# Last two output scatters issued without a wait between them, and the weight-conversion units of the second layer put into other steps of a block

## The chip, the core and the metric

The kernel runs on one core of one Trainium2 chip, as one launch. The metric is the device time of that launch in microseconds (us). Five engines work side by side, each through its own instructions in order: TensorE (PE, matmuls, with PEld for its weight loads), VectorE (DVE), ScalarE (ACT), GpSimd (POOL) and SyncE (SP). The letter q behind an engine's name means its sequencer: waits, branches and the issue of DMAs.

## The reference

Attention with two sparse masks, then a routed layer (each token goes to one of 8 experts), then a dense layer, in float32:

```
attn = softmax(where(mask, q k^T / 8, -1e9)) v           # 4 x 8 heads, 576 positions, 64 wide
x    = attn, heads side by side                          # 2304 tokens x 512
e    = argmax(x w_gate + bias[modality]);  x[e] = gate * relu(x[e] w1[e]) w2[e]
h    = x w_in                                            # 512 -> 2048
out  = where(h > 0, h, exp(min(h, 0)) - 1) w_out         # 2048 -> 512
```

The change touches only the last line, called the second layer here.

## The kernel before

**Stages.** The attention comes first (to about 100 us), then the routed layer (to about 396 us), then the second layer (to about 804 us). All matmul operands are split into a high and a low part, so one product is three matmuls: high by high, low by high, high by low. The splitting costs an ACT copy (the high part) and a DVE subtraction (the low part) for each operand tile.

**The second layer.** The tokens lie in five groups: groups 0 to 3 of 512 tokens and group 4 of 256. The 2048 hidden columns are worked in 16 chunks of 128. Ten blocks follow each other, named p = 0 to 9 here: p 0 to 4 take the groups in the order 0, 1, 4, 2, 3 with chunks 0 to 7, and p 5 to 9 take them in the order 3, 2, 1, 0, 4 with chunks 8 to 15. So each block has eight steps, c = 0 to 7, one chunk each; j counts the steps of all blocks.

A step does in program order, for each engine:
- `up`: twelve matmuls into a PSUM tile h_ps (L736 to L738), three ACT functions of it (t, e, r: L745 to L747), two DVE operations (L748, L749), the ACT copy gh (L750) and the DVE subtraction gl (L751), which are the operands of `down`;
- where they fall due: the split of a weight chunk (ACT wh L460, DVE wl L461) and of the next block's tokens (`prep`: ACT xh L449, DVE xl L450, in even steps);
- possibly one conversion unit (below);
- `down` of the step two before: twelve matmuls (six for group 4) that add into the output tiles o_ps (L772 to L774).

In the step that ends a block's `down`, the o_ps tiles are copied out of PSUM: by ACT (L781) and DVE (L783) in turn for p 0 to 4, and stored to a scratch array part_dram by a POOL DMA. Since `down` runs two steps late, the copies of block p are emitted at the end of step c = 1 of block p + 1, and the first `down` matmul of block p + 1, one step later, needs the PSUM bank that ACT's first copy frees. For p 5 to 9 DVE adds the scratch part to o_ps (L787), and a POOL indirect DMA scatters the 128 rows into the output (L788). There are 18 such scatters; each is made to wait until the one before it has landed, as all write the same array.

**Conversion units.** The weights w_in and w_out come as 64-bit numbers and are made 32-bit floats by 32 pieces of work in a software pipeline. A call of `conv.unit()` with number n stores piece n - 3 (SP DMA, L151), finishes piece n - 2 (DVE L144, L146), takes the bits of piece n - 1 apart (ACT cv_r L133, cv_a L134; DVE cv_t L136, L137) and loads piece n (SP, L119 or L122). The stages run on the same tiles, so within a unit ACT's cv_a waits for DVE's L146. Two pieces make one weight chunk. 23 units run during the routed layer, the others in the second layer, for p 0, 1, 3 and 4 (p 2 is the narrow group 4). Chunks 8 to 15 are read back by SP from step c = 3 of p = 4 on (L539), five steps ahead of their use.

**Order.** It is written out by hand: instructions stand on each engine in the order in which the code emits them, and a pool of buffers adds the waits. A wait holds everything behind it on its engine.

Of the kernel before, what the change touches and what calls it, by code (L numbers as in the profile page):

```python
# [36 lines left out]

def moe_attention_kernel(tc, q, k, v, mod, mbias, wg, w1, w2, w_in, w_out, out):
    nc = tc.nc
    with ExitStack() as ctx, tc.manual_schedule():  # L40
        const = ctx.enter_context(tc.tile_pool(name="const", bufs=1))
        dram = ctx.enter_context(tc.tile_pool(name="dram", bufs=1, space=DRAM))
        psum = ctx.enter_context(tc.tile_pool(name="psum", bufs=1, space=PSUM))
        x_dram = dram.tile([T, DM], F32, name="x_dram")
        conv = Conv(tc, dram, w_in, w_out)
        ident = const.tile([128, 128], F32, name="ident")

        def bank(tag, name, *shape):

            t = psum.tile([128, 512], F32, tag=tag, bufs={"S": 2, "T": 2, "P": 4}[tag], name=name)  # L50
            if not shape:
                return t
            n = 1
            for d in shape[1:]:
                n *= d
            t = t[0:shape[0], 0:n]
            if len(shape) == 3:
                t = t.rearrange("p (a b) -> p a b", a=shape[1])
            return t

        router = Router(tc, const, bank)
        part_dram = dram.tile([NT, 128, DM], F32, name="part_dram")
        ffn(tc, ctx, x_dram, part_dram, ident, router, conv, bank, w1, w2, out,
            lambda bg: attention(tc, bg, q, k, v, mod, mbias, wg, x_dram, ident, router, bank))


class Background:
# [29 lines left out]
class Conv:  # L97
# [51 lines left out]
    def store(self, n):  # L149
        f, part = divmod(n, 2)  # L150
        self.tc.nc.sync.dma_start(self.w[f, :, part * 512:(part + 1) * 512], self.done.pop(n))  # L151
# [245 lines left out]
def ffn(tc, ctx, x_dram, part_dram, ident, router, conv, bank, w1, w2, out, run_attention):  # L397
    nc = tc.nc
# [5 lines left out]
    idx, gate, idxd = router.idx, router.gates, router.idxd  # L404
# [114 lines left out]
    order = [0, 1, 4, 2, 3, 3, 2, 1, 0, 4]  # L519
# [27 lines left out]
    def fetch_to(g):  # L547
        while loaded[0] <= g:
            s, f = divmod(loaded[0], NCH)
            if s < NS:  # L550
                if s == len(jobs):
                    new_job(s)
                raws[loaded[0]] = fetch(jobs[s], f)
            else:
                fetch2(loaded[0] - NG)
            loaded[0] += 1

    def split_to(g):
        while splits[0] <= g:
            if splits[0] < NG:  # L560
                split_w(splits[0] % NW, raws.pop(splits[0]))
            else:
                split2(splits[0] - NG)
            splits[0] += 1
# [8 lines left out]
    def prep(p, kks=range(4)):  # L573
        s = order[p]
        for kk in kks:
            split_x(y_sb[0][:, kk, s * 512:s * 512 + widths[s]], yT[sets[p]][kk])
# [152 lines left out]
    def up(j):  # L729
        p, c = seq[j]  # L730
        i, n = where[j], widths[order[p]]
        ps = bank("ST"[j % 2], "h2_ps")[:, 0:n]
        for kk in range(4):
            a, b = (w[i][:, kk * 128:(kk + 1) * 128] for w in (WH, WL))
            yh, yl = (y[:, 0:n] for y in yT[sets[p]][kk])
            nc.tensor.matmul(ps, lhsT=a, rhs=yh, start=kk == 0, stop=False)  # L736
            nc.tensor.matmul(ps, lhsT=a, rhs=yl, start=False, stop=False)  # L737
            nc.tensor.matmul(ps, lhsT=b, rhs=yh, start=False, stop=kk == 3)  # L738

        t = e_p.tile([128, 512], F32, tag="t", name="t")[:, 0:n]  # L740
        e = e_p.tile([128, 512], F32, tag="e", bufs=1, name="e")[:, 0:n]
        r = e_p.tile([128, 512], F32, tag="r", name="r")[:, 0:n]
        gh = h_p.tile([128, 512], F32R, tag="hh", name="gh")
        gl = h_p.tile([128, 512], F32R, tag="hl", name="gl")
        nc.scalar.activation(t, ps, AF.Tanh, scale=0.5)  # L745
        nc.scalar.activation(e, ps, AF.Exp)  # L746
        nc.scalar.activation(r, ps, AF.Relu)  # L747
        nc.vector.scalar_tensor_tensor(t, e, 1.0, t, ALU.add, ALU.mult)  # L748
        nc.vector.scalar_tensor_tensor(r, t, 0.0, r, ALU.min, ALU.add)  # L749
        nc.scalar.copy(gh[:, 0:n], r)  # L750
        nc.vector.tensor_tensor(gl[:, 0:n], r, gh[:, 0:n].bitcast(F32), ALU.subtract)  # L751
        hid[j] = (gh, gl)

    parts = {}

    def load_part(p, m):

        parts[m] = xg_p.tile([128, DM], F32, tag="xg", name="part")
        nc.sync.dma_start(parts[m], part_dram[4 * order[p] + m])

    def down(j):
        p, c = seq[j]
        i, s = where[j], order[p]
        gh, gl = hid.pop(j)
        nt = widths[s] // 128
        first, last = j % HC == 0, j % HC == HC - 1
        if first:
            acc[p] = [bank("P", f"o_ps{m}") for m in range(nt)]
        for m in range(nt):
            a, b = (g[:, m * 128:(m + 1) * 128] for g in (gh, gl))  # L770
            ps = acc[p][m]
            nc.tensor.matmul(ps, lhsT=a, rhs=WH[i][:, 512:1024], start=first, stop=False)  # L772
            nc.tensor.matmul(ps, lhsT=a, rhs=WL[i][:, 512:1024], start=False, stop=False)  # L773
            nc.tensor.matmul(ps, lhsT=b, rhs=WH[i][:, 512:1024], start=False, stop=last)  # L774
            if not last:
                continue
            col = 4 * s + m
            if p < 5:
                o = xg_p.tile([128, DM], F32, tag="xg", name="o")
                if m % 2:  # L780
                    nc.scalar.copy(o, ps)  # L781
                else:
                    nc.vector.tensor_copy(o, ps)  # L783
                nc.gpsimd.dma_start(part_dram[col], o)
            else:
                o = parts.pop(m)
                nc.vector.tensor_tensor(o, ps, o, ALU.add)  # L787
                nc.gpsimd.indirect_dma_start(out, bass.IndirectOffsetOnAxis(idxd[:, col:col + 1], 0), o, None)  # L788

    fetch_to(NG + LAG - 1 + AHEAD)  # L790
    for j in range(NX + LAG):
        if j < NX:
            up(j)
            split_to(NG + j + SPLIT + 1)
            fetch_to(NG + j + AHEAD + 1)
            p, c = seq[j][0], j % HC
            if p + 1 < len(order) and sets[p + 1] != sets[p] and c % 2 == 0:
                prep(p + 1, [c // 2])
            if p < 5 and order[p] != 4 and c % 2 == 1:
                conv.unit()  # L800
            if p >= 5 and c >= 4 and c - 4 < widths[order[p]] // 128:
                load_part(p, c - 4)
        if j >= LAG:
            down(j - LAG)


def attention(tc, bg, q, k, v, mod, mbias, wg, x_dram, ident, router, bank):
# [333 lines left out]
```

## Time and profile before

| | us |
|---|---|
| median of 3 runs | 812.84 (810.42 to 813.59) |
| the profiled execution, device time | 815.83 |
| its span, first to last instruction | 814.1 |
| PE busy in the span | 775.6 (95%) |
| DVE busy | 517.0 (64%) |
| ACT busy | 397.0 (49%) |
| POOL busy | 105.3 (13%) |
| mean granted TensorE clock | 0.976 of full |

The device time is 1.73 us longer than the span. A matmul row of the timeline shows its start and its modelled length; since matmuls are pipelined, the distance from one start to the next tells more than the length. In a bracket behind a row stands how long the engine was idle before it and what ended that idle time.

### The profile page before, as it was taken

The numbers are of one execution on the slowest core, as the hardware profiler recorded it, in microseconds if no ns is written. First come the engines' busy times: TensorE is split into PE (matmuls) and PEld (weight loads), VectorE is DVE, ScalarE is ACT, GpSimd is POOL, SyncE is SP. The second block draws the span as 40 slices with busy tenths as digits, with TensorE's granted clock in tenths as the row PEclk, the third lists the DMA queues.
The fourth block names the chain that finished last, engine by engine and source line by source line (L and its number), as shares of the span: only waits on it lengthen the run. The fifth ranks groups of instructions, "written<-read, shape, count | busy, mean of one in ns | idle before, by whom it ended". The sixth has DMA issues, their size and how long they took to land.

```text
span 814.1 us, 12741 instructions
## 1 busy us (share of the span) xinstructions
PE 775.6 (95%) x4513; PEld 645.1 (79%) x4513; DVE 517.0 (64%) x1394; ACT 397.0 (49%) x759; POOL 105.3 (13%) x131
## 2 busy tenths in 40 slices
PE   7999989998999999999699899999999999999994
PEld 6899877776888888888587688788887888888884
DVE  3789878696867676765677656664467454545452
ACT  4667646422445453453466555554466444444341
POOL 4533342022002020000000101001001010101011
PEclk9999969999999999999899999999999999999998
DMA  9487692345556664555432222111133020211111
GB/s 171 116 184 179 148 239 66 107 139 153 201 188 200 203 221 157 183 181 164 148 103 79 95 74 91 39 45 75 37 103 130 1 93 11 66 39 47 57 39 64
DMA packets 100302, 94.37 MB, mean 116 GB/s; under 512 B 45433, under 2 KB 78731, under 8 KB 100235
## 3 DMA queue, kind: packets, MB, share of 16 engines
q1 hardware_dynamic: 95056, 78.79, 33.5%
q0 software_dynamic: 4480, 14.68, 5.2%
q8 instruction: 37, 0.61, 0.3%
q14 instruction: 30, 0.25, 0.1%
q10 hardware_dynamic: 699, 0.04, 0.1%
HBM read 70.95 MB, written 22.54 MB: 115 GB/s over the span
## 4 chain that ended last, share of the span: by engine, by line
PE 43%; DVE 4%; ACT 3%; issue 1%; DMA 0%; POOLq 0%; DVEq 0%; ACTq 0%
PE o_ps L772 7%; PE o_ps L774 7%; PE o_ps L773 7%; PE h_ps L736 7%; PE h_ps L737 7%; PE h_ps L738 7%; DVE r L749 1%; DVE t L748 1%; ACT gh L750 1%; DVE wl L461 1%; ACT t L745 1%; ACT e L746 1%; DVE cv_r L146 1%; ACT wh L460 0%; DVE cv_r L144 0%
## 5 line engine op out<-in xcount | busy, mean ns | idle before, releaser
L736 PE MATMUL h_ps<-xh,wh 128*128 128x512 f32 (+1 forms) x320 | 119.5, 373 | 6.8 <-DVEq L697 6.8
L748 DVE SCALAR_TENSOR_TENSOR t<-e,t 128x512 f32<-128x512 f32 (+1 forms) x80 | 51.1, 639 | 117.7 <-ACT e L746 117.7
L737 PE MATMUL h_ps<-xl,wh 128*128 128x512 f32 (+1 forms) x320 | 119.3, 373 | 0.3 <-DVE xl L450 0.3
L738 PE MATMUL h_ps<-xh,wl 128*128 128x512 f32 (+1 forms) x320 | 119.1, 372 | 0.0
L772 PE MATMUL o_ps<-wh,gh 128*128 128x512 f32 x288 | 113.9, 396 | 4.2 <-ACT o L781 4.2
L773 PE MATMUL o_ps<-wl,gh 128*128 128x512 f32 x288 | 113.4, 394 | 0.0
L774 PE MATMUL o_ps<-wh,gl 128*128 128x512 f32 x288 | 113.3, 394 | 0.0
L745 ACT ACTIVATE t<-h_ps 128x512 f32<-128x512 f32 (+1 forms) x80 | 44.3, 554 | 107.0 <-PE h_ps L738 107.0
L750 ACT CAST gh<-r 128x512 fp32r<-128x512 f32 (+1 forms) x80 | 46.2, 577 | 80.6 <-DVE r L749 80.6
L751 DVE TENSOR_TENSOR gl<-r,gh 128x512 fp32r<-128x512 f32 (+1 forms) x80 | 51.1, 639 | 51.5 <-ACT gh L750 51.5
L461 DVE TENSOR_TENSOR wl<-wraw,wh 128x1024 fp32r<-128x1024 f32 x56 | 68.6, 1225 | 13.7 <-ACT wh L460 12.4
L736 PEld LDWEIGHTS h_ps<-xh,wh 128*128 128x128 f32 x320 | 60.6, 189 | 19.3 <-issue 7.2
L737 PEld LDWEIGHTS h_ps<-xl,wh 128*128 128x128 f32 x320 | 60.7, 190 | 12.5 <-DVE xl L450 0.6
L738 PEld LDWEIGHTS h_ps<-xh,wl 128*128 128x128 f32 x320 | 60.5, 189 | 11.0
L772 PEld LDWEIGHTS o_ps<-wh,gh 128*128 128x128 f32 x288 | 54.5, 189 | 16.9 <-ACT o L781 5.1
L495 PE MATMUL y_ps<-hh,wh 128*128 128x512 f32 x160 | 64.3, 402 | 0.0
L476 PE MATMUL h_ps<-xh,wh 128*128 128x512 f32 x160 | 64.2, 401 | 0.0
L774 PEld LDWEIGHTS o_ps<-wh,gl 128*128 128x128 f32 x288 | 54.4, 189 | 12.3
L478 PE MATMUL h_ps<-xh,wl 128*128 128x512 f32 x160 | 63.6, 398 | 0.0
L773 PEld LDWEIGHTS o_ps<-wl,gh 128*128 128x128 f32 x288 | 54.5, 189 | 11.2
L477 PE MATMUL h_ps<-xl,wh 128*128 128x512 f32 x160 | 63.3, 396 | 0.0
L497 PE MATMUL y_ps<-hh,wl 128*128 128x512 f32 x160 | 62.8, 392 | 0.0
(178 smaller groups left out, 1419.4 us busy)
## 6 DMA issues: line engine op xcount, KB each, us to landing
wraw<-in_moe_w_dram SPq DMA_DIRECT2D x80, 256.0 KB
raw<-in_moe_w_in_dram SPq DMA_DIRECT2D x16, 512.0 KB
raw<-in_moe_w_out_dram SPq DMA_DIRECT2D x16, 512.0 KB
w_f<-cv_r SPq DMA_DIRECT2D x32, 256.0 KB
wraw<-w_f SPq DMA_DIRECT2D x16, 512.0 KB
part_dram<-o POOLq DMA_DIRECT2D x18, 256.0 KB, 3.5
part<-part_dram SPq DMA_DIRECT2D x18, 256.0 KB
qn<-in_q_dram SPq DMA_DIRECT2D x8, 288.0 KB
```

The costliest lines, as they stand in the source:

```text
L461: nc.vector.tensor_tensor(WL[i], raw, WH[i].bitcast(F32), ALU.subtract)
L476: nc.tensor.matmul(ps, lhsT=a, rhs=job.xh[kk], start=kk == 0, stop=False)
L477: nc.tensor.matmul(ps, lhsT=a, rhs=job.xl[kk], start=False, stop=False)
L478: nc.tensor.matmul(ps, lhsT=b, rhs=job.xh[kk], start=False, stop=kk == 3)
L495: nc.tensor.matmul(ps, lhsT=a, rhs=hh, start=f == 0, stop=False)
L497: nc.tensor.matmul(ps, lhsT=b, rhs=hh, start=False, stop=f == NCH - 1)
L736: nc.tensor.matmul(ps, lhsT=a, rhs=yh, start=kk == 0, stop=False)
L737: nc.tensor.matmul(ps, lhsT=a, rhs=yl, start=False, stop=False)
L738: nc.tensor.matmul(ps, lhsT=b, rhs=yh, start=False, stop=kk == 3)
L772: nc.tensor.matmul(ps, lhsT=a, rhs=WH[i][:, 512:1024], start=first, stop=False)
L773: nc.tensor.matmul(ps, lhsT=a, rhs=WL[i][:, 512:1024], start=False, stop=False)
L774: nc.tensor.matmul(ps, lhsT=b, rhs=WH[i][:, 512:1024], start=False, stop=last)
```

## The change

Two edits, independent of each other.

First, a unit used to run in steps c = 1, 3, 5 and 7 of the blocks p 0, 1, 3 and 4; now it runs in c = 3, 5 and 7. That is 12 calls instead of 16. Before, numbers n = 23 to 38 were called, of which the last four found nothing to do (32 pieces and three stages of lag need n up to 34). Now n = 23 to 34 are called, so the same pieces are done, and the three last calls (n = 32, 33, 34) fall into p = 4.

Second, in the last block the scatters are no longer emitted where their data is made but kept and emitted after the whole layer, outside the stretch in which the order is written by hand, and the second is declared to have no dependence on the first.

```diff
-    with ExitStack() as ctx, tc.manual_schedule():
+    with ExitStack() as ctx:
+        manual = ctx.enter_context(ExitStack())
+        manual.enter_context(tc.manual_schedule())
...
+        manual.close()
+
+        ds = [store() for store in last_stores]
+        tc.declare_no_dep(ds[1].ins, ds[0].ins, query=mybir.DependencyQuery.ANY_SYNC,
+                          reason="no two of these transfers write the same row of out")
...
-                nc.gpsimd.indirect_dma_start(out, bass.IndirectOffsetOnAxis(idxd[:, col:col + 1], 0), o, None)
+                store = lambda o=o, col=col: nc.gpsimd.indirect_dma_start(out, bass.IndirectOffsetOnAxis(idxd[:, col:col + 1], 0), o, None)
+                if p + 1 < len(order):
+                    store()
+                else:
+                    last_stores.append(store)
...
-            if p < 5 and order[p] != 4 and c % 2 == 1:
+            if p < 5 and order[p] != 4 and c in (3, 5, 7):
                 conv.unit()
```

How the instructions stand now, at the three places of which the prediction speaks. On ACT, the change from block p = 0 to p = 1, step c = 1 and the start of step c = 2 (lines of the changed kernel are 7 higher; the numbers behind o_ps are those of its tiles). Before:

```order
L745 ACTIVATE t<-h_ps 128x512
L746 ACTIVATE e<-h_ps 128x512
L747 ACTIVATE r<-h_ps 128x512
L750 CAST gh<-r 128x512
L133 ACTIVATE cv_r<-raw_5654 128x512
L134 ACTIVATE cv_a<-raw_5654 128x512
L781 COPY o<-o_ps_5424 128x512
L781 COPY o<-o_ps_5426 128x512
L745 ACTIVATE t<-h_ps 128x512
```

And in the changed kernel:

```order
L752 ACTIVATE t<-h_ps 128x512
L753 ACTIVATE e<-h_ps 128x512
L754 ACTIVATE r<-h_ps 128x512
L757 CAST gh<-r 128x512
L788 COPY o<-o_ps_5412 128x512
L788 COPY o<-o_ps_5414 128x512
L752 ACTIVATE t<-h_ps 128x512
```

The two operations of the unit (cv_r, cv_a) are gone from between gh and the two copies out of PSUM. The same holds at the start of p = 3, and in step c = 1 of p = 0 a unit is gone from behind a weight split.

On SP, the end of the conversion: loads of 64-bit weights (raw), stores of converted pieces (w_f), and the weight chunks read back (wraw). Before:

```order
L122 DMA raw_5934<-in_moe_w_out_dram 128x1024
L151 DMA w_f_66<-cv_r 128x512
L119 DMA raw_6022<-in_moe_w_in_dram 128x4x256
L151 DMA w_f_66<-cv_r 128x512
L122 DMA raw_6386<-in_moe_w_out_dram 128x1024
L151 DMA w_f_66<-cv_r 128x512 x3
L539 DMA wraw<-w_f_66 128x1024 x8
```

And in the changed kernel:

```order
L129 DMA raw_6618<-in_moe_w_out_dram 128x1024
L546 DMA wraw<-w_f_66 128x1024
L158 DMA w_f_66<-cv_r 128x512
L546 DMA wraw<-w_f_66 128x1024 x2
L158 DMA w_f_66<-cv_r 128x512
L546 DMA wraw<-w_f_66 128x1024 x2
L158 DMA w_f_66<-cv_r 128x512
L546 DMA wraw<-w_f_66 128x1024 x3
```

The last three stores now stand between the eight read-backs, where they all stood ahead of them.

On POOL, the last scatters with the waits that they carry (DMASW: a DMA of this queue, DVE: the addition). Before:

```order
L788 DMA out_dram<-part,idxd 2304x512 [waits DMASW4_49,DVE_49]
L788 DMA out_dram<-part,idxd 2304x512 [waits DMASW5_49,DVE_49]
L788 DMA out_dram<-part,idxd 2304x512 [waits DMASW6_49,DVE_49]
L1137 UNCONDITIONAL_BRANCH
L1137 ISA [waits barrier_Pool_Activation_PE_DVE_SP_gather]
```

And in the changed kernel:

```order
L795 DMA out_dram<-part,idxd 2304x512 [waits DMASW4_49,DVE_49]
L795 DMA out_dram<-part,idxd 2304x512 [waits DMASW5_49,DVE_49]
L795 DMA out_dram<-part,idxd 2304x512 [waits DVE_49]
L1150 UNCONDITIONAL_BRANCH
L1150 ISA [waits barrier_Pool_Activation_PE_DVE_SP_gather]
```

The order is the same; the last scatter has lost its wait for the one before it and keeps the one for its data.

## Rows read from the trace of the kernel before

**Rows 1.** Waits of PE, 395 to 815 us: engine, line, releaser: us, times, longest.
```profile
PE o_ps L772 <- ACT o L781: 4.2, 2, 3.2
```

**Rows 2.** PE timeline, p = 0 to 1: start, us, line, operation [idle before, releaser].
```profile
445.35 0.39 PE L738 MATMUL h_ps<-xh,wl 128*128 128x512 f32 x1
...
450.87 0.40 PE L738 MATMUL h_ps<-xh,wl 128*128 128x512 f32 x1
454.47 0.80 PE L772 MATMUL o_ps<-wh,gh 128*128 128x512 f32 x1 [3.20 <-ACT o L781]
...
458.75 0.39 PE L736 MATMUL h_ps<-xh,wh 128*128 128x512 f32 x1
```

**Rows 3.** ACT timeline of the same place.
```profile
447.94 0.59 ACT L745 ACTIVATE t<-h_ps 128x512 f32<-128x512 f32 x1
...
451.10 0.66 ACT L133 ACTIVATE cv_r<-raw 128x512 int32<-128x512 uint32 x1
453.27 0.67 ACT L134 ACTIVATE cv_a<-raw 128x512 f32<-128x512 f32 x1 [1.52 <-DVE cv_r L146]
453.85 1.05 ACT L781 COPY o<-o_ps 128x512 f32<-128x512 f32 x2
```

**Rows 4.** Windows: busy us of PE, PEld, DVE, ACT, POOL; granted clock, DMA share, GB/s.
```profile
454.10:457.50 3.40, 3.03 (x7) 2.45 (x8) 2.79 (x5) 2.33 (x6) 2.24 (x4) 0.50 0.75 243
...
523.00:527.00 4.00, 3.00 (x13) 2.15 (x12) 3.38 (x6) 2.62 (x5) 0.94 (x2) 1.00 0.19 70
```

**Rows 5.** PE timeline, p = 2 to 3.
```profile
523.92 0.40 PE L774 MATMUL o_ps<-wh,gl 128*128 128x512 f32 x1
525.32 0.50 PE L772 MATMUL o_ps<-wh,gh 128*128 128x512 f32 x1 [1.00 <-ACT o L781]
```

**Rows 6.** ACT timeline of the same place.
```profile
521.95 0.68 ACT L133 ACTIVATE cv_r<-raw 128x512 int32<-128x512 uint32 x1
...
524.71 0.57 ACT L781 COPY o<-o_ps 128x512 f32<-128x512 f32 x1
```

**Rows 7.** PE timeline, `up` of the first step of p = 1.
```profile
438.72 0.49 PE L736 MATMUL h_ps<-xh,wh 128*128 128x512 f32 x1
439.53 0.50 PE L737 MATMUL h_ps<-xl,wh 128*128 128x512 f32 x1 [0.31 <-DVE xl L450]
```

**Rows 8.** ACT timeline, the unit in step c = 1 of p = 0.
```profile
408.59 0.67 ACT L133 ACTIVATE cv_r<-raw 128x512 int32<-128x512 uint32 x1
...
411.88 0.58 ACT L745 ACTIVATE t<-h_ps 128x512 f32<-128x512 f32 x1
```

**Rows 9.** ACT timeline, p = 3 to 4, where no unit stands in c = 1.
```profile
562.91 0.60 ACT L745 ACTIVATE t<-h_ps 128x512 f32<-128x512 f32 x1 [2.26 <-PE h_ps L738]
...
566.07 1.07 ACT L781 COPY o<-o_ps 128x512 f32<-128x512 f32 x2
```

**Rows 10.** PE timeline of the same place.
```profile
565.47 0.39 PE L736 MATMUL h_ps<-xh,wh 128*128 128x512 f32 x1
...
568.23 0.40 PE L772 MATMUL o_ps<-wh,gh 128*128 128x512 f32 x1
```

**Rows 11.** POOL timeline, 800 to 815 us.
```profile
804.14 0.97 POOL L788 DMA_INDIRECT out_dram<-part,idxd  x1 [5.97 <-DVE part L787]
807.63 0.97 POOL L788 DMA_INDIRECT out_dram<-part,idxd  x1 [2.51 <-DMA out_dram<-part,idxd]
```

**Rows 12.** DVE timeline, 803 to 805 us.
```profile
803.17 1.37 DVE L787 TENSOR_TENSOR part<-o_ps,part 128x512 f32<-128x512 f32 x2 [0.88 <-PE o_ps L774]
```

**Rows 13.** POOL timeline, gathers of the routed layer with no wait between them.
```profile
247.84 0.96 POOL L441 DMA_INDIRECT xg<-x_dram,idx  x1 [0.30 <-issue]
249.10 1.02 POOL L441 DMA_INDIRECT xg<-x_dram,idx  x1 [0.30 <-issue]
```

**Rows 14.** POOL's drains: duration in ns min/median/max, first and last start.
```profile
L1137 POOLq DRAIN  x3: 40/113/5850, 807.4 to 813.8; - x3
```

**Rows 15.** The gathers' tile: issue to landing.
```profile
DMA to landing us min/median/max: 3.2/5.7/8.0
```

More of the change, by code (lines that the diff above doesn't have):

```diff
@@ L62, in moe_attention_kernel @@
         part_dram = dram.tile([NT, 128, DM], F32, name="part_dram")
-        ffn(tc, ctx, x_dram, part_dram, ident, router, conv, bank, w1, w2, out,
+        last_stores = ffn(tc, ctx, x_dram, part_dram, ident, router, conv, bank, w1, w2, out,
             lambda bg: attention(tc, bg, q, k, v, mod, mbias, wg, x_dram, ident, router, bank))
+        manual.close()
+        ds = [store() for store in last_stores]
+        tc.declare_no_dep(ds[1].ins, ds[0].ins, query=mybir.DependencyQuery.ANY_SYNC,
+                          reason="no two of these transfers write the same row of out")
 class Background:
@@ L752, in up @@
         hid[j] = (gh, gl)
-    parts = {}
+    parts, last_stores = {}, []
     def load_part(p, m):
@@ L804, in ffn @@
             down(j - LAG)
+    return last_stores
 def attention(tc, bg, q, k, v, mod, mbias, wg, x_dram, ident, router, bank):
```

## The prediction

> **What bounds the kernel now.** I read the waits of PE first, since PE is busy for 95% of the span. In the second layer PE stops almost nowhere, but two of its waits are for the same thing, ACT's copies of o_ps, 4.2 us in all [rows 1]. Then I read the PE timeline at these two places and the ACT timeline beside it. The reader is to see that PE has finished one step and wants the first `down` matmul of the next block, and that ACT reaches the copy that frees the bank only after a conversion unit. Last I read the end of the span on POOL and DVE: PE and DVE are done, and the two last scatters follow each other with a wait between them.
>
> The normal pitch, from a stretch without a stop: twelve matmuls from 565.47 to 568.23, 2.76 us, so 0.230 us each [rows 10]. All losses below are start-to-start distances beyond that pitch.
>
> **Part 1, the units out of c = 1: what it removes.**
>
> Place A, the step from p = 0 to p = 1. PE starts a matmul at 450.87 and the next only at 454.47 [rows 2]: 3.60 - 0.23 = 3.37 us lost. ACT shows why: the unit's cv_r begins at 451.10, cv_a waits 1.52 us for the DVE half of the unit and begins at 453.27, and the first copy begins at 453.85, 2.75 us after the unit began [rows 3]. PE starts 0.62 us after that copy does. Behind the stop the granted clock is 0.50, the lower of its two levels [rows 4], and the twelve `down` matmuls from 454.47 to 458.75 [rows 2] take 4.28 us in place of 2.76: another 1.52 us.
>
> Without this unit the copy stands where cv_r stood, at 451.10 at the latest, and PE would go on at 451.72 instead of 451.10: a stop of 0.62 us at most. It is shorter still, since the other removed unit, in c = 1 of p = 0, lies upstream on the same chain. There ACT and DVE spend 408.59 to 411.88 on it, 3.29 us until the next step's t [rows 8], and from there on ACT is behind PE: the `up` of step c = 1 of p = 1 has its last matmul at 445.35, so its t could begin at about 445.8, and it begins at 447.94 [rows 2, 3]. Working the chain through with 3.29 us less, that t is no longer late, and everything behind it moves up by 2.1 us: the copy begins at about 449.0, before PE wants the bank. So I take the whole 3.37 us and the whole 1.52 us.
>
> The Trainium skill speaks of the clock in "TensorE: Matmul & The Clock Gate", section "Part 1: The HAM clock gate (the "warmup" mystery)": the low level is the default, activity lifts it, and the moments at which the chip decides run free of the kernel's start. In this trace the stop of 3.37 us has the low clock behind it and the shorter one at place B does not, so a stop is not always paid twice. If other executions of the kernel before escape the low clock at place A, as that rule allows, the sum would be 1.52 us smaller for them.
>
> Place B, the step from p = 2 to p = 3. PE starts at 523.92 and then at 525.32 [rows 5]: 1.40 - 0.23 = 1.17 us, at full clock [rows 4]. The copy begins at 524.71, behind a unit that began at 521.95 [rows 6]. Without it the copy begins at 521.95, and PE could go on at 522.57, while it wants to at 524.15. Taken whole: 1.17 us.
>
> Place C, the `up` of the first step of p = 1. It waits for the low part of the split tokens, 439.53 - 438.72 - 0.23 = 0.58 us [rows 7]. That split stands on the late chain behind the unit of p = 0, c = 1; 3.29 us earlier it is there in time. Taken whole: 0.58 us.
>
> At p = 4 the call in c = 1 had nothing to do before, so nothing is gained there, and the step from p = 3 to p = 4 is the model of what A and B become: the copy begins at 566.07, and PE wants the bank at 568.23 [rows 9, 10] and does not stop.
>
> Sum of part 1: 3.37 + 1.52 + 1.17 + 0.58 = 6.64 us. From below, if each of the two stops keeps the 0.62 us that a copy needs, 1.24 us of it stay and the sum is 5.40.
>
> **Part 1: what it adds and moves.** No piece of work is added. The pieces move by one to three units, and real work comes into p = 4: bits and finish at c = 3, a finish at c = 5, a store at c = 7. The only one with ACT work costs 2.75 to 3.29 us of the chain [rows 3, 8]. In this stretch ACT is idle 2.26 us per step while it waits for PE [rows 9], so ACT falls behind by at most about 1.0 us and has it back one step later, a step before the weight splits of this block start and five before the next copies. I cost it at nothing. If that cover were gone, ACT would be a unit late at the step from p = 4 to p = 5, and the price would be a stop like B, 1.17 us.
>
> On SP the last three stores now stand between the read-backs. None waits long: the DVE half of each store is done one call earlier, four steps or two before it, and a read-back comes five steps ahead of its use. The last piece is stored in c = 7 of p = 4, the chunk that holds it is read back three steps later; at 24 matmuls of 0.230 us a step that is 16.6 us. I cost it at nothing.
>
> **Part 2, the last scatters.** Before, the first begins on POOL at 804.14 and the second at 807.63, after waiting 2.51 us for the first to land [rows 11]. The data of the second is there at 803.17 + 1.37 = 804.54 [rows 12]. Two indirect DMAs of POOL with no wait between them begin 1.26 us after each other [rows 13]. So the second begins at 804.14 + 1.26 = 805.40, that is 2.23 us earlier.
>
> The trace does not show two scatters in flight, nor what the queue's drain waits for. It ends at 807.40 + 5.85 = 813.25 [rows 14], 5.62 us after the second scatter begins, and only the closing barrier follows it. If it follows that scatter, in start or landing, all of the 2.23 us come through. From below: if it hangs on something else, nothing comes; if the second one lands late beside the first, as the slowest gather did (8.0 us [rows 15], where 2.51 + 0.97 = 3.48 is the most that the first scatter takes here), up to 4.5 us are lost, 2.3 more than gained. From above: if the second needed only its data and the 0.28 us after which the first scatter followed its own addition, it would begin at 804.82 and 2.81 us come. I take 2.23, as the nearest row is of the same operation on the same queue.
>
> **The sum.** 6.64 + 2.23 = 8.87 us. The profiled execution took 815.83 us, so it would take 806.96. The median of the runs shown is 812.84, 2.99 below the profiled one. The losses above come from the order of instructions, not from the profiler, so I take the same 8.87 off the median: 803.97, in short 804.0 us.
>
> **The rivals.**
>
> 1. *Only the blocks gain.* The drain at the end keeps its time, and the scatter's 2.23 us are hidden. For it: the drain is entered before the second scatter begins, and it ends well after it. Against it: nothing else on that queue is left to wait for. Time: 812.84 - 6.64 = 806.2. Chance 0.12.
>
> 2. *The gain is eaten in part.* The second scatter lands late (2.3 us worse than before, so 812.84 - 6.64 + 2.3 = 808.5), or the stops keep 1.24 us, the low clock was not in the other runs (1.52), and p = 4 to 5 gets a stop like B (1.17), so 812.84 - 8.87 + 3.9 = 807.9. For it: none of these is shown either way. Against it: each has room in the rows above. Time about 808 to 809.5. Chance 0.11.
>
> 3. *The change doesn't do what it says*: another wait stood behind the unit on ACT, such as the buffers of o, and the copies stay late. Then A and B stay, and only C and the scatter come: 812.84 - 2.8 = 810.0. Against it: the first copy begins as soon as the unit's last ACT operation lets it, 0.58 us after cv_a's start [rows 3]. Chance 0.03.
>
> 4. *Slower.* Chunk 15 is converted too late. It is stored one block later than before, and its read-back must wait for that store, SP's other loads behind it. PE stops at c = 7 of p = 5, and the low clock follows as at A. The cover is at least the 16.6 us above, and the delay must also eat the 8.87 gained: from about 25.5 us of delay of that store on, the kernel is slower than before. At 27.5 us it would take 812.84 - 8.87 + 10.9 = 814.9, and with the 1.52 of a low clock 816.4. For it: the margin shrinks from a block and more to three steps. Against it: nothing on SP is ever that late in this stretch. Chance 0.02.
>
> **How the numbers follow.** The forecast, all terms whole to within about 2 us, has 0.72. I count 0.5%, 4.06 us, as what a measurement of this kernel can tell from no change, so faster means below 808.8. The forecast and rival 1 are faster (0.84), rival 2 about for a third of its chance (0.03): 0.87. The rest of rival 2 and rival 3 are within 0.5%, with a little for runs that lie higher: 0.10. Rival 4 and the unknown: 0.03. The range: the fastest run before, 810.42, with the upper end of the scatter's gain gives 801.0, and rival 2 ends at about 809; 800.8 to 809.0 leaves out some 0.1.
>
> **What would show it.** Right: PE goes from the last `up` matmul of c = 2 into the first `down` matmul at the normal pitch at A and B, with ACT's copy directly behind gh; the waits of PE on the copies are gone, and the low clock at the start of p = 1 with them; the two last scatters begin about 1.26 us apart, and the drain ends about 5.6 us after the second. Wrong: a stop of more than 0.6 us at A or B, a new stop of PE in p = 4 or 5, or a drain that ends later than 8 us after PE's last matmul.

## The result, and the profile after

| | before | changed |
|---|---|---|
| median of 5 runs, us | 811.66 (810.42 to 813.59) | 803.72 (803.27 to 805.89) |
| ratio to before, 95% interval | | 0.9891 (0.9864 to 0.9918) |
| profiled execution, device time | 815.83 | 803.72 |
| its span | 814.1 | 802.0 |
| first to last L772 matmul (`down`) | 406.09 to 802.97 = 396.88 | 403.17 to 793.08 = 389.90 |
| last matmul to the end of the span | 803.43 to 814.08 = 10.65 | 793.53 to 801.97 = 8.44 |
| all before the first `down` | 406.09 | 403.17 |

The kernel is 1.1% faster; 803.72 us was measured where 804.0 was forecast. The ratio puts the gain at 8.8 us (6.7 to 11.0); the two medians of the table lie 7.9 us apart, inside that interval.

The two stretches that the change touches gained 6.98 and 2.21 us in the trace, 9.19 in all. The span fell by 12.1: the other 2.9 us lie ahead of the second layer's first `down`, where both kernels have the same code. That part ends between 400.4 and 408.3 us in the ten profiled executions of this study, and in two executions of the same changed kernel at 403.17 and 405.50. So it is scatter from one execution to the next, and the reason why the sections below compare stretches of the second layer rather than spans.

The waits of PE from 390 to 800 us in the changed kernel (engine, line, releaser: us, times, longest), its whole list:

```profile
PE h_ps L743 <- DVEq L704: 6.8, 1, 6.8
```

The wait on ACT's copies [rows 1] and the one on the split tokens [rows 7] are gone; what is left is the start of the second layer, which was there before too.

Place A after the change, PE and then ACT, each by start and length in us:

```profile
447.14 0.39 PE L745 MATMUL h_ps<-xh,wl 128*128 128x512 f32 x1
447.37 0.40 PE L779 MATMUL o_ps<-wh,gh 128*128 128x512 f32 x1
```
```profile
442.05 0.60 ACT L752 ACTIVATE t<-h_ps 128x512 f32<-128x512 f32 x1 [0.38 <-PE h_ps L745]
...
444.69 0.62 ACT L757 CAST gh<-r 128x512 fp32r<-128x512 f32 x1 [1.06 <-DVE r L756]
445.22 1.07 ACT L788 COPY o<-o_ps 128x512 f32<-128x512 f32 x2
```

PE goes from `up` into `down` at the normal pitch, 0.23 us, where it lost 3.37 us [rows 2]. ACT's copy stands directly behind gh, and the bracket in ACT's first row is the other half of the story: ACT waits for PE again, so its chain is no longer behind. In [rows 3] the same operation began with no wait, as it was already late. The chain catches up only just at this step: where the units alone are moved, and in the repeat of the changed kernel, the same operation follows the one before it by 0.03 us (at 441.54 and 444.38), and PE does not stop there either.

Place B, ACT and PE:

```profile
513.35 0.58 ACT L788 COPY o<-o_ps 128x512 f32<-128x512 f32 x1
```
```profile
515.33 0.39 PE L781 MATMUL o_ps<-wh,gl 128*128 128x512 f32 x1
515.55 0.40 PE L779 MATMUL o_ps<-wh,gh 128*128 128x512 f32 x1
```

The copy is there 2.2 us before PE wants the bank; the 1.17 us of [rows 5] are gone. The granted clock over the two long stretches of the layer (busy us of PE, PEld, DVE, ACT, POOL, then the clock):

```profile
403.00:600.00 197.00, 197.00 (x903) 162.73 (x902) 124.40 (x195) 110.56 (x212) 7.56 (x14) 1.00 0.24 81
600.00:793.00 193.00, 193.00 (x885) 159.31 (x884) 96.76 (x152) 88.89 (x174) 18.09 (x20) 1.00 0.17 55
```

Full throughout, where the start of p = 1 ran at 0.50 [rows 4].

The end, on DVE, on POOL, and POOL's drains (ns, min/median/max, first and last start):

```profile
793.28 1.37 DVE L794 TENSOR_TENSOR part<-o_ps,part 128x512 f32<-128x512 f32 x2 [0.89 <-PE o_ps L781]
```
```profile
794.24 0.97 POOL L795 DMA_INDIRECT out_dram<-part,idxd  x1 [5.89 <-DVE part L794]
795.52 0.96 POOL L795 DMA_INDIRECT out_dram<-part,idxd  x1 [0.30 <-issue]
```
```profile
L1150 POOLq DRAIN  x3: 40/113/6450, 794.7 to 801.7; - x3
```

The scatters begin 1.27 us apart instead of 3.49 [rows 11], and the idle time before the second is the 0.30 us of issue that stood between the gathers [rows 13]. The long drain ends at 801.14, 5.62 us after the second scatter begins, as it did before [rows 14].

### The profile page after: what moved, and what is told of

It reads as the page before. It is cut to its first block, busy times and chain, and to the rows that moved or that the text cites. A ratio compares the mean times of both kernels' runs of the same rounds, so it can differ in the third digit from the quotient of the medians.

```text
span 802.0 us, 12740 instructions
## 1 busy us (share of the span) xinstructions
PE 770.6 (96%) x4513; PEld 642.2 (80%) x4513; DVE 516.4 (64%) x1394; ACT 396.2 (49%) x759; POOL 104.8 (13%) x131
## 4 chain that ended last, share of the span: by engine, by line
PE 50%; POOLq 0%; POOL 0%; DVE 0%; issue 0%
PE h_ps L743 8%; PE h_ps L744 8%; PE h_ps L745 8%; PE o_ps L779 8%; PE o_ps L780 8%; PE o_ps L781 8%; POOLq L1150 0%; POOL out_dram L795 0%; DVE part L794 0%
## 5 line engine op out<-in xcount | busy, mean ns | idle before, releaser
L781 PEld LDWEIGHTS o_ps<-wh,gl 128*128 128x128 f32 x288 | 54.1, 188 | 12.1
L503 PE MATMUL y_ps<-hl,wh 128*128 128x512 f32 x160 | 63.4, 396 | 0.0
```

What stands on the lines that cost most here:

```text
L503: nc.tensor.matmul(ps, lhsT=a, rhs=hl, start=False, stop=False)
```

## The experiments

Eight kernels ran. "L772 stretch" is the time from the first to the last matmul of that line, and "the tail" the time from the last matmul to the end of the span. A repeat of the changed kernel comes last. In the kernel with the first tile earlier the last matmuls stand in another order, so its stretch is not put beside the others; its section compares the matmuls from the first `down` to the last.

| kernel | L772 stretch | tail | scatters apart |
|---|---|---|---|
| before | 396.88 | 10.65 | 3.49 |
| changed | 389.90 | 8.44 | 1.27 |
| units only | 389.92 | 10.66 | 3.49 |
| scatters only | 396.74 | 8.44 | 1.27 |
| no unit in c = 1 of p = 0 | 392.50 | 10.66 | 3.48 |
| no unit in c = 1 of p = 1 | 392.90 | 10.64 | 3.48 |
| last store later | 389.92 | 8.45 | 1.27 |
| traffic beside the scatters | 389.92 | 10.84 | 1.27 |
| first tile earlier | | 7.97 | 1.27 |
| the change again | 389.93 | 8.45 | 1.27 |

**The units alone.** The kernel before with one line changed:

```diff
-            if p < 5 and order[p] != 4 and c % 2 == 1:
+            if p < 5 and order[p] != 4 and c in (3, 5, 7):
```

Expected: 

> The units moved, the scatters as before. My theory: the stops at A (3.37 us and 1.52 us of low clock), B (1.17) and C (0.58) go, 6.64 us in all, so 811.7 - 6.6 = 805.0 us; the last two scatters still begin about 3.5 us apart. Rival 3 (something else than the unit holds the copies): A and B stay, about 811 us.

Measured: ratio 0.9924 (0.9895 to 0.9952) to the kernel before on the same chip (814.06 us median there), 6.2 us less (3.9 to 8.5). PE waits for no copy in the second layer, and the L772 stretch is that of the changed kernel to 0.02 us. The tail is that of before. Rival 3 is out: nothing but the units held the copies.

**The scatters alone.** The changed kernel with that line put back:

```diff
-            if p < 5 and order[p] != 4 and c in (3, 5, 7):
+            if p < 5 and order[p] != 4 and c % 2 == 1:
```

Expected: 

> The last two scatters without a wait, the units as before. My theory: they begin 1.27 us apart, the drain ends 5.62 us after the second begins, 2.2 us saved: 811.7 - 2.2 = 809.5 us; the stops at A, B and C stay at 3.4, 1.2 and 0.6 us and the low clock stands behind A. Rival 1 (the drain hides it): 811.7 us.

Measured: ratio 0.9965 (0.9945 to 0.9985), 2.8 us less (1.2 to 4.5) with 2.2 expected. The tail is 8.44 us, all of the gain is there. Its PE waits, 386 to 805 us:

```profile
PE h_ps L743 <- DVEq L704: 6.8, 1, 6.8
PE o_ps L779 <- ACT o L788: 4.2, 2, 3.2
PE h_ps L744 <- DVE xl L457: 0.3, 1, 0.3
```

These are the waits of before, to the tenth [rows 1, 7]. The two edits are independent, and rival 1 is out: the drain does not hide the scatter. The clock at place A, as windows:

```profile
452.00:457.70 5.70, 2.51 (x12) 1.71 (x11) 4.65 (x8) 3.71 (x8) 0.60 (x1) 1.00 0.17 54
457.80:461.10 3.30, 3.30 (x9) 2.51 (x9) 2.41 (x4) 1.40 (x3) 1.53 (x3) 0.50 1.01 368
```

PE stops here from 452.78 to 456.37, as long as before, and goes on at full clock; the low level comes later, on matmuls that run without a gap. Before, it was low when PE went on. The stop was followed by the low clock in both executions, though after different times. Place C lost 0.44 us in this execution where it had lost 0.58, so the late chain does not cost exactly the same each time.

**One unit of four, upstream of place A.** The kernel before, without the unit in c = 1 of p = 0:

```diff
-            if p < 5 and order[p] != 4 and c % 2 == 1:
+            if p < 5 and order[p] != 4 and c % 2 == 1 and (p, c) != (0, 1):
```

Expected: 

> Of the four edits of units only one: no unit in c = 1 of p = 0 (one more piece then comes in p = 4). My theory of a late chain: C goes; at A the unit in c = 1 of p = 1 still stands ahead of the copy, but begins 2 to 3 us earlier, so the stop shrinks from 3.37 to about 1.2 us, with no low clock behind it; B stays at 1.2. Rival (the stop at A is the price of the unit beside it alone, the one upstream has no part in it): A stays at 3.4 us, with the low clock.

Measured: place C is gone. At A the unit beside the copy still stands, on ACT:

```profile
443.43 0.62 ACT L750 CAST gh<-r 128x512 fp32r<-128x512 f32 x1 [1.07 <-DVE r L749]
443.96 0.67 ACT L133 ACTIVATE cv_r<-raw 128x512 int32<-128x512 uint32 x1
446.13 0.68 ACT L134 ACTIVATE cv_a<-raw 128x512 f32<-128x512 f32 x1 [1.50 <-DVE cv_r L146]
446.72 1.04 ACT L781 COPY o<-o_ps 128x512 f32<-128x512 f32 x2
```
```profile
445.88 0.40 PE L738 MATMUL h_ps<-xh,wl 128*128 128x512 f32 x1
447.33 0.50 PE L772 MATMUL o_ps<-wh,gh 128*128 128x512 f32 x1 [1.05 <-ACT o L781]
```

The unit takes 2.76 us, as in [rows 3], yet the stop is 1.45 - 0.23 = 1.22 us, with 1.2 expected, and the clock stays at 1.00 behind it. B keeps its 1.17. So 2.15 us of the stop at A, and the low clock, went with a unit that stands eight steps earlier.

That unit is not the only one upstream. In the kernel before, the chain that ends in the stop at A runs from 400.78 to 454.47 through ACT and DVE alone, with no matmul between, and it holds the cv_a of five units, of c = 1, 3, 5 and 7 of p = 0 and of c = 1 of p = 1 (start, us, what):

```profile
411.30 0.68 ACT cv_a L134
...
423.56 0.67 ACT cv_a L134
...
434.32 0.68 ACT cv_a L134
...
443.91 0.67 ACT cv_a L134
...
453.27 0.67 ACT cv_a L134
453.95 0.48 ACT o L781
454.47 0.80 PE o_ps L772
```

Whether the stop would have shrunk as much without the unit in c = 3, 5 or 7 of p = 0 instead was not tried.

**The other one.** The same, but with the unit of p = 1 left out:

```diff
-            if p < 5 and order[p] != 4 and c % 2 == 1:
+            if p < 5 and order[p] != 4 and c % 2 == 1 and (p, c) != (1, 1):
```

Expected: 

> Only no unit in c = 1 of p = 1. My theory: C stays at 0.6 us, A shrinks to 0.6 to 0.8 us, as the copy then stands where cv_r stood and the chain is still late by about 2 us; no low clock; B stays at 1.2. Rival (A is the price of the unit beside it alone): A goes whole. Other rival (A is the price of the lateness upstream alone): A stays above 2.5 us.

Measured, PE and ACT at A:

```profile
445.19 0.40 PE L738 MATMUL h_ps<-xh,wl 128*128 128x512 f32 x1
446.05 0.50 PE L772 MATMUL o_ps<-wh,gh 128*128 128x512 f32 x1 [0.46 <-ACT o L781]
```
```profile
442.25 0.59 ACT L745 ACTIVATE t<-h_ps 128x512 f32<-128x512 f32 x1
...
445.41 1.07 ACT L781 COPY o<-o_ps 128x512 f32<-128x512 f32 x2
```

The copy now follows gh at once, and still PE loses 0.86 - 0.23 = 0.63 us, since the chain is late: t begins with no wait in front of it. C stays (433.03 to 433.83, 0.8 us as in [rows 7]), and so does B with 1.17. The stop at A is the product of both units: with either one removed the low clock did not come, in one execution each, and both must go to end the stop. Both rivals of these two runs (one unit alone has the whole price) are out.

**The last store one block boundary later.** The changed kernel with

```diff
-            if p < 5 and order[p] != 4 and c in (3, 5, 7):
+            if (p, c) in ((4, 3), (4, 7), (5, 1)) or p < 4 and order[p] != 4 and c in (3, 5, 7):
```

Expected: 

> The changed kernel with the last piece stored one block boundary later still: of p = 4 the calls are c = 3 and 7, and the last call is c = 1 of p = 5, so the last chunk is read back one step after its store instead of three. My theory (the margin of 16.6 us is cover, and a step of 5.5 us is enough too): no new stop of PE, first to last down matmul in 389.9 us as in the changed kernel. Rival 4 (a late store holds SP's loads and PE stops): a stop at c = 5 to 7 of p = 5, some us longer.

Measured: no new stop, and a stretch of 389.92 us. SP shows how near the store and the read-back now are (the last store, then the last read-back):

```profile
598.76 0.43 SPq L158 DMA_DIRECT2D w_f<-cv_r  x1
603.80 0.32 SPq L546 DMA_DIRECT2D wraw<-w_f  x1
```

They are 5.0 us apart, and that is enough, but with little to spare. The first row below is a wait of SP that the changed kernel does not have, the read-back's for the store (us, times, longest); the second is the DVE operation that frees the buffer of the read-back:

```profile
SPq L546 <- DMA w_f<-cv_r: 3.8, 1, 3.8
```
```profile
602.55 1.23 DVE L468 TENSOR_TENSOR wl<-wraw,wh 128x1024 fp32r<-128x1024 f32 x1 [0.26 <-ACT wh L467]
```

SP had issued the store by 599.19, so the store had landed by about 603.0, and the buffer came free at 603.78, some 0.7 us later. In the changed kernel the store is at 586.73 and the last read-back begins 16.0 us later. Rival 4 needed a delay of more than 25 us; this run delays the store by 11, so it measures the cover and could not have shown the rival. What speaks against rival 4 is the changed kernel itself, in which PE does not stop in p = 4 or 5 for more than 0.11 us.

**Traffic beside the last scatters.** The changed kernel, with 2 MB more written by SP at the end:

```diff
...
+        for i in range(8):
+            nc.sync.dma_start(spare[i], last_o[1])
...
```

Expected: 

> The changed kernel, and beside the last two scatters SP writes the last output tile eight times to a scratch array, 2 MB that the reference doesn't have. The landing of the last scatter is late by some us; its start is not. If POOL's drain follows the start of the last scatter, it still ends 5.62 us after it; if it follows the landing, it ends about 2.9 us after that and moves with it. I hold both for possible, landing at 0.6.

Measured, POOL and its drains, and the window with the traffic:

```profile
797.12 0.97 POOL L799 DMA_INDIRECT out_dram<-part,idxd  x1 [0.30 <-issue]
```
```profile
L1155 POOLq DRAIN  x3: 40/113/7587, 796.3 to 805.7; - x3
```
```profile
796.00:802.00 6.00, 0.00 (x0) 0.00 (x0) 0.25 (x1) 0.00 (x0) 1.79 (x2) 0.67 0.83 302
```

The last scatter landed 4.42 us after its start; in the changed kernel it took 2.71. The drain ended at 803.88, 6.76 us after the start instead of 5.62, and 2.34 us after the landing instead of 2.91. So, in this one run, it is not a fixed time after the start, and not after the landing either: it moved by 1.14 us where the landing moved by 1.71. That part of the question stays open. The tail of 10.84 us says nothing of it: in this kernel SP, which waits for its own writes, reaches its closing drain only at 805.1, behind POOL's, which ended at 803.88. The verdict is not touched: the drain moves with the scatter, and in all nine other executions it ended 5.62 or 5.63 us after the second one began, whether that had waited or not.

**The first tile earlier.** The changed kernel, with the last twelve matmuls in another order, so that the first output tile is done five matmuls ahead of the second:

```diff
...
+    for j, m, k in [(y, 0, 0), (y, 0, 1), (y, 0, 2), (y, 1, 0), (z, 0, 0), (z, 0, 1), (z, 0, 2)]:
+        piece(j, m, k)
+    finish(0)
+    for j, m, k in [(y, 1, 1), (y, 1, 2), (z, 1, 0), (z, 1, 1), (z, 1, 2)]:
+        piece(j, m, k)
+    finish(1)
...
```

(y and z are the last two steps, m the tile, k the three products; `finish` does the addition and keeps the scatter.)

Expected: 

> The changed kernel with the last twelve matmuls in another order: the first output tile is done five matmuls before the second, not three. The first scatter begins about 1.1 us before the second's data is there, so the pitch of 1.27 us between them hides more of itself: the second begins about 0.3 us after its data, where it was 0.87. From the last matmul to the end about 0.5 us less than in the changed kernel, some 0.1 us of it lost to waits of PE. Rival (the drain has a length of its own): no gain. Too small for the times: same as the changed kernel, about 0.989 of before.

Measured: 801.93 us, ratio 0.9866 (0.9823 to 0.9908). DVE and POOL:

```profile
791.52 0.69 DVE L827 TENSOR_TENSOR part<-o_ps,part 128x512 f32<-128x512 f32 x1 [0.60 <-PE o_ps L821]
792.68 0.69 DVE L827 TENSOR_TENSOR part<-o_ps,part 128x512 f32<-128x512 f32 x1 [0.47 <-PE o_ps L821]
```
```profile
792.49 0.97 POOL L828 DMA_INDIRECT out_dram<-part,idxd  x1 [6.27 <-DVE part L827]
793.76 0.97 POOL L828 DMA_INDIRECT out_dram<-part,idxd  x1 [0.31 <-issue]
```

The second scatter begins 0.39 us after its data is there, with 0.3 expected, where it was 0.87; the tail is 7.97 us, 0.47 less, of which PE gives back 0.2 (390.57 us from the first `down` matmul to the last matmul, where the changed kernel has 390.36). The pitch of the two scatters, 1.27 us, still decides by a hair. A gain of 0.26 us in the trace is no more than the times can tell: the intervals of this kernel and of the next overlap widely.

**The change again**, beside the last one on the same chip.

Expected: 

> The changed kernel once more on the chip of the kernel beside it: 8.9 us below before, ratio 0.989; the same 389.9 us from the first to the last down matmul, scatters 1.27 us apart, drain 5.62 us after the second.

Measured: ratio 0.9895 (0.9857 to 0.9932), and the same stretch and tail to 0.03 us.

## Why the prediction was right

The bound was read rightly. In the second layer PE loses more than 0.11 us at three places alone, and each of the three went for the reason that was given. That the time itself came out within 0.3 us of the forecast is in part luck: the forecast started from a median of 812.84, five runs gave 811.66, and the runs of one kernel lie 2.6 to 3.2 us apart. The stretches of the trace are the closer test.

- *Part 1.* Predicted 6.64 us, measured 6.98 in the trace (units alone: 6.96), and 6.2 (3.9 to 8.5) in the times. The 0.34 us more are gaps of A, B and C that the sum left out, since it counted one gap at each: ahead of C, 438.32 to 438.72, PE lost another 0.17, and the second matmul behind C and behind B comes 0.11 late each. These make 0.39. Against them the low clock cost 1.48 and not 1.52, since twelve matmuls at the same place take 2.80 us in the changed kernel (447.37 to 450.17) where the sum took 2.76; that leaves 0.35. After the change the small gaps are gone as well.
- *Place A.* Both halves of the working were shown apart: with the upstream unit gone, 1.22 us of stop remain; with the unit beside it gone, 0.63 (the bound of 0.62 for a copy in that place). The term of 1.52 us for the low clock came through, within 0.2 us also in the execution in which the low clock came later. The alternative, that other executions escape it, was not seen: two of two executions with the long stop had it, which is few, and it stood behind none of the five stops of 1.40 to 1.45 us from start to start (B in four executions, A in one).
- *What the moved units cost.* Nothing, as predicted. PE shows no stop in p = 4. The only one left in the layer is 0.11 us, twice, at the step from p = 4 to p = 5, and it is there in every kernel of the table, before included. SP's margin came out at 16.0 us with 16.6 worked out, and 5.0 us is enough. The sum left out that the read-back waits for the store to land, 3.8 us in the run with the late store, so the cover that the store really has is smaller than the 16.6 us by about that much.
- *Part 2.* Predicted 2.23 us, measured 2.21. The gathers were the right model: the pitch of two scatters is 1.27 us, of two gathers 1.26.
- *The rivals.* 1 and 3 were each tried and fell; 4 fell with the changed kernel itself. Of rival 2 the part with the second scatter landing late did not come: it landed 2.71 us after its start, with the first one in flight beside it. With 2 MB of other writes beside it, it took 4.42, so a late landing can come from other traffic, of which there was none here.

What was not known and not needed: what POOL's drain waits for. The range was wider than it had to be, because this was priced from nothing to a loss of 2.3 us.

## What to carry to other kernels

When PE waits for another engine, look at what that engine did just before, but also whether it was waiting for PE then: an engine that begins step after step without a wait for PE's result is late or only just on time, and the price of a piece of work on it may be paid eight steps later. Here two units of 3.3 and 2.8 us, on engines busy for 49% (ACT) and 64% (DVE) of the time, cost 4.9 us together at the one step where a copy had to be on time. Work that is free in most steps belongs in a step behind which nothing urgent stands. A second transfer at the very end that writes other rows than the first need not wait for it; what remains is the pitch at which the queue issues.

## What the runs showed of the hardware that was not expected

- The low clock does not begin at a fixed time after the stop ahead of it: at the same stop of 3.36 us it began as PE went on in one execution (454.12, with PE on at 454.47) and 1.4 us later in another (457.76, with PE on at 456.37). The cost was the same within 0.2 us.
- POOL's drain at the end of the program lasts until 2.3 to 2.9 us after the last scatter has landed, while SP is through with its own waits at 798.87, 2.3 us before the drain ends at 801.14. In the changed kernel the drain, not the transfer, sets the end; only with the 2 MB beside it did SP end last.
- The time up to the second layer, the same code in all ten kernels, differed by up to 7.9 us between executions (400.4 to 408.3). Between the two profiled executions of the changed kernel the spans differ by 2.37 us, of which 2.33 lie there. From the first `down` matmul to the last, the five executions without a stop agree to 0.03 us, and the two with the long stop to 0.14.
